# Moving one group of small matmuls behind the KV stage, and three more no-op matmuls, in a fused attention and FFN kernel

## Chip, cores, metric

One core of a Trainium2 chip. The time is the device time of one execution in microseconds (us); lower is better. Profiles are of one execution each. The profiled execution of the kernel before was a slow one, with a granted clock of the tensor engine of 0.655 and 1249.2 us.

## The reference

```python
def reference(A_x, A_wqkv, A_wo, B_x, B_w_gate, B_w_up, B_w_down, c, w_mod):
    # _A_ref: qkv = x @ wqkv, 32 heads of 32; phi(t) = where(t > 0, t + 1, exp(t)) + 1e-6
    #   kv = sum_s phi(k) v ; z = sum_s phi(k) ; o = phi(q) kv / (phi(q) z + 1e-6) ; o @ wo
    # _B_ref: (silu(x @ w_gate) * (x @ w_up)) @ w_down
    x = A_x                                               # 2048 x 1024
    mod = (_silu(c) @ w_mod).reshape(c.shape[0], 6, 1, -1)
    sa, ca, ga, sb, cb, gb = ...                          # six rows of 1024
    h = _layernorm(x, axis=-1) * (1 + ca) + sa
    x = x + ga * _A_ref(h, A_wqkv, A_wo)
    h = _layernorm(x, axis=-1) * (1 + cb) + sb
    x = x + gb * _B_ref(h, B_w_gate, B_w_up, B_w_down)
    return x
```

The last four modulation rows (ga, gb, sb, cb) are not needed until the end of the attention half. The kernel makes them, in two groups, in between other matmuls.

## The kernel before

The 2048 rows are worked in four chunks of 512 (`sc` 0 to 3). A chunk's K stage is eight groups of eight matmuls (128x128 weights, 512 columns). The KV stage of the chunk before, 128 matmuls of 64 columns, stands behind the first two groups.

```python
    def kv_phase(sc):                       # 128 matmuls of 64 columns
        kvp = acc_b("kvp", (HG, 2, DH))
        for hg in range(HG):
            for t in range(STC):
                for i in range(HPC):
                    mm(kvp[i * DH:(i + 1) * DH, hg, :, :], lhsT=pks[sc][...], rhs=v_ones(...), ...)
        ...

    def mod_load(cols):                     # four loads of 1 MB
        blks = []
        for lo in cols:
            t = big("wml", [DC, NB])
            nc.sync.dma_start(out=t[:], in_=wm_v[:, :, lo:lo + NB])
            blks.append(t)
        return blks

    def mod_rows(blks):                     # 32 matmuls, four at a time side by side
        ps = acc_b("modr")
        for j in range(DC):
            for g in range(4):
                mm(ps[32 * g:32 * g + 32, :], lhsT=sc32[:, j, :], rhs=blks[g][:, j, :], ...)
        ...

    def keep_warm(acc, n):                  # no-ops: they multiply by zeros
        for _ in range(n):
            mm(acc[:], lhsT=sel[:, 0, :], rhs=sel[:], start=True, stop=True)
    ...
    keep_warm(spare, 9)
    ...                                     # first modulation rows, transposes, more no-ops
    for sc in range(NSC):
        if sc > 0:
            k_phase(sc, 0, 2)
            kv_phase(sc - 1)
            k_phase(sc, 2, 4)
            if sc >= 2:
                mod_spread(sc - 2, mod_rows(blks))
            k_phase(sc, 4, 8)
            if sc == 1:
                blks = mod_load([2 * D, 2 * D + NB, 5 * D, 5 * D + NB])
            if sc == 2:
                blks = mod_load([3 * D, 3 * D + NB, 4 * D, 4 * D + NB])
        v_phase(sc)
        ...                                 # layernorm of the next chunk, behind phi of K group 3
```

In the profile, `kvp` is the KV stage, `modr` the modulation rows of the second kind, `wml` their weights, `sel` the no-ops' operand, and `acc<-wk,hT` the K stage.

## Time and profile before

| | before |
|---|---|
| time, median of 3 (range) | 837.8 us (837.59 to 838.01) |
| profiled execution | 1249.2 us, a slow one |

The first fence has lines of the profile's page: busy time of each engine with its share of the span, and the chain that ended last by engine. The second is the view of cores. The third is the waits of the tensor engine: total us, times, longest us.

```profile
PE 1232.9 (99%) x4560; PEld 468.0 (37%) x4641; DVE 309.5 (25%) x598; ACT 169.3 (14%) x253; POOL 60.8 (5%) x167
...
PE 99%; issue 1%; DVE 0%
```

```profile
core 0: 1249.2 us, clock 0.655
```

```profile
PE acc L98 <- issue: 5.1, 26, 0.2
PE acc L98 <- DVE sel L429: 1.2, 1, 1.2
```

PE is the limit from end to end, and it waits for 6.3 us in all. But this is an execution at 0.655 of the clock, half as long again as the timed ones. Here are its KV stages of chunks 1 and 2 in the timeline of PE (start us, us, engine, line, operation, tiles, shapes, count, and in brackets the idle time just before):

```profile
86.15 1.42 PE L98 MATMUL kvp<-v,pk 128*32 128x64 bf16 x128
87.51 15.83 PE L98 MATMUL acc<-wk,hT 128*128 128x512 bf16 x47
...
129.35 1.42 PE L98 MATMUL kvp<-v,pk 128*32 128x64 bf16 x128
130.97 5.05 PE L98 MATMUL acc<-wk,hT 128*128 128x512 bf16 x15 [0.20 <-issue]
135.95 2.77 PE L98 MATMUL modr<-wml,sc 128*32 128x512 bf16 x32
```

### The profile page before, as it was taken

How to read it: one execution, taken by the hardware profiler on the slowest of the kernel's cores; microseconds unless marked ns; L12 is line 12 of the kernel's file. 1: busy time of each engine (PE TensorE's matmuls, PEld its weight loads, DVE VectorE, ACT ScalarE, POOL GpSimd, SP SyncE). 2: the span in 40 equal slices, each digit the busy share in tenths (PEclk: the TensorE clock that was granted, in tenths of full speed). 3: DMA queues.
4: the chain of work that ended last, by engine and by line, in shares of the span. 5: the costliest groups of instructions: out<-in, count | busy, mean ns of one | idle time of the engine just before them, and what ended most of it. 6: DMA issues, size and time to landing. Idle time of an engine off the chain costs nothing.

```text
span 1249.2 us, 11163 instructions
## 1 busy us (share of the span) xinstructions
PE 1232.9 (99%) x4560; PEld 468.0 (37%) x4641; DVE 309.5 (25%) x598; ACT 169.3 (14%) x253; POOL 60.8 (5%) x167
## 2 busy tenths in 40 slices
PE   9999999999999999999999999999999999999998
PEld 3333333333433333333333333333333333333333
DVE  4443531564221222311111232111112221111111
ACT  2423322322011101001111000011100001111000
POOL 1101200110300001000000000000000000000000
PEclk7666666666666666666666666666666666666666
DMA  9444520139452414253140231623204218300011
GB/s 344 120 152 135 148 65 1 36 108 307 111 149 87 167 47 160 64 165 105 34 140 30 72 122 58 218 69 98 71 1 143 76 49 271 124 11 1 13 38 34
DMA packets 126756, 129.33 MB, mean 104 GB/s; under 512 B 34033, under 2 KB 108273, under 8 KB 126193
## 3 DMA queue, kind: packets, MB, share of 16 engines
q1 hardware_dynamic: 122368, 114.97, 29.3%
q0 software_dynamic: 4048, 13.25, 3.4%
q8 instruction: 36, 0.59, 0.2%
q10 hardware_dynamic: 288, 0.40, 0.1%
q14 instruction: 16, 0.12, 0.0%
HBM read 108.53 MB, written 12.72 MB: 97 GB/s over the span
## 4 chain that ended last, share of the span: by engine, by line
PE 99%; issue 1%; DVE 0%
PE acc L98 90%; PE a_ps L98 7%; PE modr L98 0%; PE kvp L98 0%; PE mod_ps L98 0%; PE tp L101 0%; PE den L98 0%; PE wf L98 0%; DVE e L638 0%; DVE ob L641 0%; DVE sel L429 0%; DVE neg_half L172 0%
## 5 line engine op out<-in xcount | busy, mean ns | idle before, releaser
L98 PE MATMUL acc<-h2T,wgu 128*128 128x512 bf16 x1756 | 580.8, 513 | 5.0 <-issue 1.6
L98 PEld LDWEIGHTS <-wgu 128*128 128x128 bf16 x1792 | 217.1, 121 | 367.4 <-issue 367.1
L98 PE MATMUL acc<-wd,gu 128*128 128x512 bf16 (+2 forms) x908 | 293.5, 503 | 2.4 <-issue 1.0
L617 DVE TENSOR_TENSOR gu<-acc,e 128x512 bf16<-128x512 f32 x112 | 77.5, 692 | 497.9 <-PE acc L98 475.4
L98 PEld LDWEIGHTS <-gu 128*128 128x128 bf16 x924 | 111.0, 121 | 182.1 <-issue 178.6
L616 ACT ACTIVATE e<-acc 128x512 f32<-128x512 f32 x112 | 66.9, 597 | 607.0 <-PE acc L98 588.5
L98 PEld LDWEIGHTS <-hT 128*128 128x128 bf16 x512 | 61.6, 121 | 102.9 <-issue 100.6
L98 PE MATMUL a_ps<-wo,pq 128*128 128x512 bf16 x250 | 85.1, 512 | 0.6
L98 PE MATMUL acc<-wk,hT 128*128 128x512 bf16 x248 | 83.7, 513 | 1.3 <-issue 0.8
L98 PE MATMUL acc<-hT,wq 128*128 128x512 bf16 x247 | 83.0, 512 | 1.6 <-issue 1.4
L98 PE MATMUL acc<-wv,hT 128*128 128x512 bf16 x251 | 83.5, 513 | 0.8 <-issue 0.4
L638 DVE TENSOR_TENSOR e<-acc,gb_bc 128x512 f32<-128x512 f32 (+2 forms) x33 | 22.3, 676 | 232.8 <-PE acc L98 219.7
L288 ACT ACTIVATE eb<-acc 128x512 bf16<-128x512 f32 x64 | 38.0, 597 | 131.8 <-PE acc L98 131.0
L289 DVE TENSOR_SCALAR eb<-eb 128x512 bf16<-128x512 bf16 x64 | 18.8, 293 | 134.0 <-ACT eb L288 133.9
L98 PEld LDWEIGHTS <-pq 128*128 128x128 bf16 x256 | 30.8, 120 | 52.6 <-issue 52.6
L98 PEld LDWEIGHTS <-wq 128*128 128x128 bf16 x256 | 29.9, 119 | 51.5 <-issue 51.2
L227 ACT ACTIVATE xn<-x,nmr,rstd 128x1024 bf16<-128x1024 f32 x16 | 19.8, 1239 | 191.9 <-POOL nmr L225 191.9
L585 POOL DMA_DIRECT2D x_scratch<-x x16 | 9.7, 608 | 657.5 <-DVE x L578 657.5
L578 DVE TENSOR_TENSOR x<-a_ps,x_sb 128x512 f32<-128x512 f32 x32 | 22.1, 692 | 35.7 <-PE a_ps L98 33.3
L326 ACT CAST v<-acc 128x512 bf16<-128x512 f32 x32 | 18.7, 584 | 57.0 <-PE acc L98 55.4
L211 POOL TENSOR_TENSOR rstd<-veps,neg_half 128x1 f32<-128x1 f32 x32 | 17.8, 555 | 103.0 <-DVE veps L209 102.9
L641 DVE TENSOR_TENSOR ob<-e,x1r 128x512 bf16<-128x512 f32 (+2 forms) x33 | 22.3, 675 | 1.0
(76 smaller groups left out, 268.4 us busy)
## 6 DMA issues: line engine op xcount, KB each, us to landing
wgu<-in_B_w_gate_dram SPq DMA_DIRECT2D x28, 1024.0 KB, 5.5
wgu<-in_B_w_up_dram SPq DMA_DIRECT2D x28, 1024.0 KB, 6.0
x_sb<-in_A_x_dram SPq DMA_DIRECT2D x32, 256.0 KB, 6.0
wml<-in_w_mod_dram SPq DMA_DIRECT2D x8, 1024.0 KB, 8.5
x_scratch<-x POOLq DMA_DIRECT2D x16, 512.0 KB, 2.9
x1r<-x_scratch SPq DMA_DIRECT2D x31, 256.0 KB, 2.8
wd<-in_B_w_down_dram SPq DMA_DIRECT2D x7, 1024.0 KB, 5.7
rbc<-rden_scratch POOLq DMA_DIRECT2D x16, 256.0 KB, 4.6
```

The costliest lines, as they stand in the source:

```text
L98: return tc.keep_in_program_order(nc.tensor.matmul(out, lhsT=lhsT, rhs=rhs, start=start, stop=stop))
L211: nc.gpsimd.tensor_tensor(out=rstd[:, 0:n], in0=veps[:, 0:n], in1=neg_half[:].to_broadcast([P, n]), op=ALU.pow)
L227: nc.scalar.activation(out=dst, in_=src, func=ACT.Identity, bias=nmr[:], scale=rstd[:, 0:1])
L288: nc.scalar.activation(out=e[:], in_=acc, func=ACT.Exp)
L289: nc.vector.tensor_scalar(out=e[:], in0=e[:], scalar1=1.0, scalar2=PHI_EPS, op0=ALU.min, op1=ALU.add)
L326: nc.scalar.copy(out=v[:, t * D + nb * NB:t * D + (nb + 1) * NB], in_=acc[:])
L578: nc.vector.tensor_tensor(out=x1[:, ns], in0=a_ps[:], in1=x_t[:, ns], op=ALU.add)
L585: nc.gpsimd.dma_start(out=x1_dram[st * P:(st + 1) * P, :], in_=x1[:])
L616: nc.scalar.activation(out=sg[:], in_=ps[0][:], func=ACT.Silu)
L617: gm = nc.vector.tensor_tensor(out=guT[sc][f // GPT][:, f % GPT, :], in0=ps[1][:], in1=sg[:], op=ALU.mult)
L638: nc.vector.tensor_tensor(out=yt, in0=y_ps, in1=gb_bc[:, ns], op=ALU.mult)
L641: nc.vector.tensor_tensor(out=ob, in0=yt, in1=x1r, op=ALU.add)
```

## The change

The three no-ops were to fill gaps among the first loads. The first group of modulation rows was to go behind the KV stage, both of them being made of narrow matmuls, and to be done earlier.

```diff
-        keep_warm(spare, 2)
+        keep_warm(spare, 4)
         pe_transpose_tile(hT, xns[2], 2)
         mod_rows_a(2)
-        keep_warm(spare, 5)
+        keep_warm(spare, 6)
         mod_rows_a(3)
 ...
             k_phase(sc, 0, 2)
             kv_phase(sc - 1)
+            if sc == 2:
+                mod_spread(0, mod_rows(blks))
             k_phase(sc, 2, 4)
-            if sc >= 2:
-                mod_spread(sc - 2, mod_rows(blks))
+            if sc == 3:
+                mod_spread(1, mod_rows(blks))
             k_phase(sc, 4, 8)
```

## The prediction

> **What bounds it.** The tensor engine, start to end: PE 1232.9 of 1249.2 us (99%) on the page, a chain of waits that is 99% PE, and only 6.3 us of waits of PE, the longest 1.2. But this profile is a slow execution: granted clock 0.655 (view of cores), while timed runs take 837.8. Estimate for full clock: PE part (1249-16-3) x 0.655 = 806 us, 16 us of start, 3 of tail[...]: 832 to 835. So at most 3 to 6 us of PE stalls hide in the timed runs, which caps any gain.
>
> **What the change does.** (a) Three more no-op 128x512 matmuls: two before the third input tile's transposes, one before the last modulation rows. (b) The 32 column-tiled matmuls of the first modulation rows move two K groups earlier, directly behind the 128 KV matmuls. The order of instructions shows the same loads in the same SP order, and DVE, ACT and POOL reordered around chunk 2.
>
> **(a), costed.** The first no-ops take 0.427 us each (timeline)[...]; later ones 0.33 to 0.38[...]. In the trace the third tile's normalisation ends at 11.86 us and its transposes start at 11.91; at full clock PE is free for about 0.5 us before, so two no-ops (0.43) cost nothing. The last rows begin at 14.88, right as five no-ops end; their weights land by about 13.6 (7.8 after the issue at 5.8). At full clock the no-ops end near 13.9, so the sixth costs up to 0.2 us. [...]
>
> **(b), costed.** PE work is unchanged: 1.42 (KV) + 2.77 us (rows). The 0.20 us gap between KV and the next K group may go: -0.1. The cost is on DVE: the next chunk's layernorm may start only after the phi of K group 3. Before, the rows (about 1.8 us at full clock) stood between groups 3 and 4 and gave DVE a window with no evacuation; after, the window lies where layernorm is not yet allowed. Four phis (0.98 each) plus statistics (about 1.65 a tile) are 10.5 us of DVE against 6.9 of PE. Chunk 3's normalised input comes about 1.8 us later relative to PE. In the slow trace it is modulated by 156.5 and used at 169.9; at full clock I reckon 2 to 4 us of slack before, 0.5 to 2.5 after: just enough, as in chunk 1, which has this pattern already. The gate rows' earlier landing buys nothing: the multiplication of wo waits for wo's own load.
>
> **Prediction: 837.7 us, 8 in 10 between 836.0 and 839.3.** Faster by over 2%: 0.01; within 2%: 0.98; slower: 0.01.
>
> **What shows it.** PE still 99% busy; first real K matmul within 0.3 us of before; rows directly after KV with no idle; chunk 3's statistics begin about 1.8 us (fast) or 2.8 (slow) later relative to the end of the K stage; no PE wait at chunk 3's K stage; the chain stays PE.
>
> **What would make it wrong.** If the timed runs lose the full tensor clock in the first 16 us, which the slow profile hides, the no-ops could win 1 to 3 us. If chunk 3's input is already late at full clock, (b) costs up to 2 us. A fast profile would decide.

Its sum for full clock came to 832 to 835 us with a term of about 7 us that does not scale. That term is cut: the terms that stand, 806, 16 and 3, come to 825, and the 3 to 6 us of hidden stalls rested on the longer sum. The forecast of 837.7 does not use the sum; it lies 0.1 under the timed 837.8. In the profile after, the no-ops start 0.22 us apart from 5.19 us on.

## More of the kernel before

Only fast ones are compared.

Every matmul is two instructions, a weight load and the multiplication (4644 of each on the page after). So a KV stage is 256 instructions.

## The result, and the profile after

| | before | after |
|---|---|---|
| time, median of 4 (range) | 837.69 us (837.27 to 838.01) | 839.49 us (839.28 to 839.62) |
| ratio, 95% interval | | 1.0022 (1.0004 to 1.0039) |
| span of a profile at full clock | 836.0 us (run e0) | 837.4 us |

Ratios are the mean time of one kernel's fast runs over that of the other's of the same rounds, so not quite the ratio of the medians. The change costs 1.8 us, 0.2%. The prediction was 837.7, at most 839.3.

Lines of the page after: busy time, the chain, and the DMA queue that carries instructions (packets, MB, share of 16 engines' time).

```profile
PE 829.2 (99%) x4644; PEld 378.9 (45%) x4644; DVE 308.1 (37%) x598; ACT 169.0 (20%) x253; POOL 61.1 (7%) x167
...
q8 instruction: 36, 0.59, 0.3%
...
PE 98%; DMA 1%; DVE 0%; issue 0%; SPq 0%; ACT 0%
```

The view of cores and the waits of PE:

```profile
core 0: 837.4 us, clock 1.000
```

```profile
PE mod_ps L98 <- DMA wme<-in_w_mod_dram: 1.7, 2, 1.4
PE acc L98 <- DVE sel L429: 1.2, 1, 1.2
PE modr L98 <- issue: 1.1, 1, 1.1
PE acc L98 <- issue: 0.9, 1, 0.9
```

The wait for the first weights (`mod_ps`) is at the start of the kernel, and the kernel before has it too at full clock (2.0 us in run e0). Two others are new against the slow profile, both called "issue": for nothing that the profile shows. The timeline of PE says where they are:

```profile
61.79 1.22 PE L98 MATMUL kvp<-v,pk 128*32 128x64 bf16 x128
62.94 1.90 PE L98 MATMUL acc<-wk,hT 128*128 128x512 bf16 x8
65.73 8.79 PE L98 MATMUL acc<-wk,hT 128*128 128x512 bf16 x40 [0.89 <-issue]
...
91.72 1.22 PE L98 MATMUL kvp<-v,pk 128*32 128x64 bf16 x128
92.75 0.63 PE L98 MATMUL modr<-wml,sc 128*32 128x512 bf16 x8
94.43 1.48 PE L98 MATMUL modr<-wml,sc 128*32 128x512 bf16 x24 [1.05 <-issue]
```

Both stand 8 matmuls behind a KV stage. The second is in the middle of the modulation rows, which read four loads (their last packet began at 65.46 us) and write one accumulator, so no data can be missing there. This trace has every matmul's record (4644, of as many weight loads). Counted from the first no-op, 957 matmuls and weight loads have begun before the first idle stretch and 1468 before the second. One semaphore wait of PE's sequencer lies between, so they are 512 instructions apart, twice 256. In the packed traces of all runs that idle here, the count is the same: 479 weight loads have begun before the idle stretch of chunk 1 and 734 before that of chunk 2, whatever work stands there.

And 0.59 MB in 36 packets are 16 KB each; 36 times 256 is 9216, and PE's matmuls and weight loads are 9288. In the packet records of the changed kernel each of the 36 has 16384 bytes, and they come 254 of PE's instructions apart in the mean (209 have begun at the first, at 17.87 us, 9103 at the last, at 819.93). With the 512 between the idle stretches, I take one packet for a block of 256 instructions of PE's program. In the packet records of the trace one instruction packet runs from 63.30 to 64.39 and one from 92.05 to 93.02; PE resumes 1.34 and 1.41 us after their ends. A short window of the DMA view around the first (63.2 to 64.5 us: packets, MB, share) shows it among the loads:

```profile
q1 hardware_dynamic: 204, 0.20, 47.3%
q8 instruction: 1, 0.02, 5.2%
```

So the theory (F in the runs): PE's program is fetched a block ahead. In the changed kernel the packet of the block that PE needed after instruction 957 began when 945 had begun (63.30 us), and the next one at 67.35 us, when 973 had begun, so after that border. How much of its program PE can hold, no run tests. The 256 short instructions of a KV stage last 1.15 us, and a block takes 2.4 us from the start of its packet until PE goes on with it (2.3 to 2.9 in all the traces in which PE waits). A border that falls just behind the start of a KV stage leaves too little work until the next. The rivals: D, my prediction's, that the layernorm of the next chunk comes late; W, that the no-ops matter by their time or by the rate of PE's early matmuls (in the changed kernel the first eight no-ops start 0.43 us apart, those from 5.19 us on 0.22); later S, that the sequencer asks late whatever the DMA queues hold.

### The profile page after: what moved, and what is told of

Read it like the earlier page. It is cut to its first block, busy times and chain, and to the rows that moved or that the text cites. A ratio compares the mean times of both kernels' runs of the same rounds, so it can differ in the third digit from the quotient of the medians.

```text
span 837.4 us, 11251 instructions
## 1 busy us (share of the span) xinstructions
PE 829.2 (99%) x4644; PEld 378.9 (45%) x4644; DVE 308.1 (37%) x598; ACT 169.0 (20%) x253; POOL 61.1 (7%) x167
## 4 chain that ended last, share of the span: by engine, by line
PE 98%; DMA 1%; DVE 0%; issue 0%; SPq 0%; ACT 0%
PE acc L98 89%; PE a_ps L98 7%; DMA wme<-in_w_mod_dram 1%; PE kvp L98 1%; PE modr L98 0%; PE mod_ps L98 0%; PE den L98 0%; PE tp L101 0%; SPq L120 0%; DVE wo L550 0%; PE wf L98 0%; SPq L134 0%; DVE pq L291 0%; ACT eb L288 0%; DVE eb L289 0%
## 5 line engine op out<-in xcount | busy, mean ns | idle before, releaser
L98 PE MATMUL acc<-h2T,wgu 128*128 128x512 bf16 x1792 | 387.6, 379 | 0.0
L98 PEld LDWEIGHTS <-wgu 128*128 128x128 bf16 x1792 | 175.2, 98 | 211.3
L98 PE MATMUL acc<-wd,gu 128*128 128x512 bf16 (+2 forms) x924 | 196.1, 373 | 0.0
L619 DVE TENSOR_TENSOR gu<-acc,e 128x512 bf16<-128x512 f32 x112 | 77.5, 692 | 299.2 <-PE acc L98 299.2
L98 PEld LDWEIGHTS <-gu 128*128 128x128 bf16 x924 | 89.3, 98 | 104.5
L98 PEld LDWEIGHTS <-hT 128*128 128x128 bf16 x512 | 49.7, 98 | 60.9 <-issue 1.6
L98 PE MATMUL acc<-wk,hT 128*128 128x512 bf16 x256 | 57.1, 379 | 0.9 <-issue 0.9
L98 PE MATMUL a_ps<-wo,pq 128*128 128x512 bf16 x256 | 57.4, 379 | 0.0
L98 PE MATMUL acc<-hT,wq 128*128 128x512 bf16 x256 | 56.8, 379 | 0.0
L98 PE MATMUL acc<-wv,hT 128*128 128x512 bf16 x256 | 55.9, 379 | 0.0
L581 DVE BATCH_NORM_STATS2 stats<-x 128x6 f32<-128x512 f32 x32 | 22.2, 695 | 1.1
```

What stands on the lines that cost most here:

```text
L98: return tc.keep_in_program_order(nc.tensor.matmul(out, lhsT=lhsT, rhs=rhs, start=start, stop=stop))
L581: nc.vector.bn_stats(out=stats[:, nb, :], in_=x1[:, ns])
L619: gm = nc.vector.tensor_tensor(out=guT[sc][f // GPT][:, f % GPT, :], in0=ps[1][:], in1=sg[:], op=ALU.mult)
```

## The experiments

All ten kernels gave correct results. The runs had 5 rounds, with the kernel before in each; its medians were 837.75 (e0 to e3), 837.83 (e4 to e7) and 837.75 (e8, e9). The intervals are about 0.13% each way. So the verdicts on parts of a microsecond rest on the idle stretches in the traces, and the times confirm their sum; by the times alone, e1, e7 and e8 are not clear of the kernel before. Traces of the runs miss a few matmul records, one at a time; a count of 7 or 15 with 0.16 us idle behind it is such a place (e0's in chunk 2, for one) and is given as "none".

| run | what | median us | ratio (95%) | idle in chunk 1 | idle in chunk 2 |
|---|---|---|---|---|---|
| e0 | before | 837.49 | 0.9997 (0.9985 to 1.001) | 0.43 | none |
| e1 | no-ops alone | 838.64 | 1.001 (0.9998 to 1.0023) | 1.07 | none |
| e2 | rows alone | 838.93 | 1.0014 (1.0001 to 1.0026) | 0.56 | 0.93 |
| e3 | after, borders moved by 96 | 837.26 | 0.9994 (0.998 to 1.0007) | none | none |
| e4 | before, borders moved by 20 | 842.62 | 1.0057 (1.0044 to 1.0069) | 2.93 | 1.3 (1.61 shown, one record missing) |
| e5 | before, borders moved by 96 | 837.36 | 0.9997 (0.9985 to 1.001) | none | none |
| e6 | the same, at a later place | 837.54 | 0.9996 (0.9984 to 1.0009) | none | none |
| e7 | after, three first no-ops fewer | 838.61 | 1.001 (0.9997 to 1.0024) | 0.52 | 1.24 |
| e8 | after, first loads later | 838.00 | 1.0004 (0.9991 to 1.0016) | none | 0.55 |
| e9 | after, both groups of loads later | 837.34 | 1.0 (0.9986 to 1.0013) | none | none |

### e0: the kernel before, at full clock

No edit.

> The kernel before again, for a trace at full clock. Theory F (instruction fetch: the tensor engine reads its program in blocks of 256 instructions, one block ahead, and the 256 short instructions of a KV stage use up a block faster than the next one comes): 837.7 us; in chunk 1 an idle stretch of about 0.3 us some 11 matmuls after the KV stage; none after the KV stage of chunk 2. Rival D (the layernorm of the next chunk is late, as I predicted): no idle stretch behind the KV stages at all, and more than 0.5 us of slack before the K stage of chunk 3.

```profile
61.84 1.22 PE L98 MATMUL kvp<-v,pk 128*32 128x64 bf16 x128
63.00 2.55 PE L98 MATMUL acc<-wk,hT 128*128 128x512 bf16 x10
65.97 8.15 PE L98 MATMUL acc<-wk,hT 128*128 128x512 bf16 x37 [0.43 <-issue]
...
91.31 1.22 PE L98 MATMUL kvp<-v,pk 128*32 128x64 bf16 x128
92.69 3.40 PE L98 MATMUL acc<-wk,hT 128*128 128x512 bf16 x15 [0.16 <-DMA wml<-in_w_mod_dram]
96.03 1.91 PE L98 MATMUL modr<-wml,sc 128*32 128x512 bf16 x32
```

As F expected; its blocks are the 16 KB packets above, 254 instructions from one to the next. The kernel before loses 0.43 us at the same count of instructions: its KV stage begins six earlier, so the border falls 11 matmuls behind it (10 recorded). The slow profile had nothing there, and its packet records say why: the same block's packet runs from 82.56 to 83.92 us, before the KV stage begins at 86.15, the modulation loads being over by 77.5. So it is with chunk 2 (125.33 to 126.56, KV stage at 129.35). PE was slow and the loads were not (their 1 KB records take 46 ns in both traces, median), so here the fetch met empty queues; in e0 the packet begins 1.4 us after the start of the KV stage.

The traces' idle stretches account for the spans: 0.89 + 1.05 after, 0.43 before, a difference of 1.51 us, against 837.4 - 836.0 = 1.4 us. The medians differ by 1.8: the profiled run was the fastest of the kernel after (839.28) and the slowest of e0 (837.86).

### e1: the no-ops alone

```diff
-        keep_warm(spare, 2)
+        keep_warm(spare, 4)
 ...
-        keep_warm(spare, 5)
+        keep_warm(spare, 6)
```

> The three no-ops alone. Theory F: six more instructions ahead move every block border six instructions earlier against the work, so chunk 1 idles about 0.9 us, 8 matmuls after its KV stage, instead of 0.3; chunk 2 does not idle; 838.3 to 838.6 us with up to 0.2 us in the first 16 us. Rival D: at most 0.2 us over before. Rival W (warmth of the tensor clock): equal to or under before.

```profile
61.88 1.22 PE L98 MATMUL kvp<-v,pk 128*32 128x64 bf16 x128
63.03 1.90 PE L98 MATMUL acc<-wk,hT 128*128 128x512 bf16 x7
66.01 8.79 PE L98 MATMUL acc<-wk,hT 128*128 128x512 bf16 x40 [1.07 <-DVE eb L289]
```

838.64 us, 0.9 over before and just over the range given. The no-ops cost nothing where they stand: the first K matmul begins at 15.62 us against 15.58 in e0. They cost 47 us later, by moving the program six instructions against the borders of its blocks. That the profile names DVE as what ended this wait is an inference from what happened at that moment; the same wait is "issue" in other runs.

### e2: the rows alone

```diff
+            if sc == 2:
+                mod_spread(0, mod_rows(blks))
             k_phase(sc, 2, 4)
-            if sc >= 2:
-                mod_spread(sc - 2, mod_rows(blks))
+            if sc == 3:
+                mod_spread(1, mod_rows(blks))
```

> The moved modulation rows alone. Theory F: chunk 1 as before (0.3 us), and an idle stretch of about 0.9 us inside the rows of chunk 2, after 11 of their 32 matmuls; 838.4 to 838.8 us. Rival D: 0 to 2 us over before, and what idles is the start of chunk 3's K stage, not the rows.

```profile
91.39 1.22 PE L98 MATMUL kvp<-v,pk 128*32 128x64 bf16 x128
92.43 0.83 PE L98 MATMUL modr<-wml,sc 128*32 128x512 bf16 x11
94.19 1.47 PE L98 MATMUL modr<-wml,sc 128*32 128x512 bf16 x21 [0.93 <-issue]
```

838.93 us, 0.1 over the range given, with the idle stretch after 11 rows, as expected. Before, 11 K matmuls (2.4 us at 0.216 each, as the 64 of a V stage take 13.81 us in the changed kernel) stood between the KV stage and this border and covered the fetch. Eleven rows last 0.83 us and do not. Rival D falls: PE does not wait at the K stage of chunk 3.

### e3: the changed kernel with its borders moved

```diff
-    def keep_warm(acc, n):
+    def keep_warm(acc, n, w=NB):
         for _ in range(n):
-            mm(acc[:], lhsT=sel[:, 0, :], rhs=sel[:], start=True, stop=True)
+            mm(acc[:, 0:w], lhsT=sel[:, 0, :], rhs=sel[:].rearrange("p h e -> p (h e)")[:, 0:w], start=True, stop=True)
 ...
-    keep_warm(spare, 9)
+    keep_warm(spare, 57, 81)
```

> The changed kernel with its first nine no-ops of 512 columns made into 57 of 81 columns: nearly the same columns, 96 more instructions in the queue, which puts the block borders into the middle of each KV stage. Theory F: both idle stretches (0.89 us in chunk 1, 1.05 us inside the rows) are gone and the time is 837.3 to 837.8 us. Rival D, or any theory in which the rows' place or the no-ops' time costs: 839.3 to 839.7 us, as the changed kernel.

```profile
62.05 1.22 PE L98 MATMUL kvp<-v,pk 128*32 128x64 bf16 x128
63.21 10.53 PE L98 MATMUL acc<-wk,hT 128*128 128x512 bf16 x47
...
91.97 1.92 PE L98 MATMUL modr<-wml,sc 128*32 128x512 bf16 x32
```

837.26 us: all of the loss is gone, with the rows and the no-ops where the change put them. Only the first nine no-ops are cut smaller.

### e4: the kernel before with its borders moved by 20

```diff
-    keep_warm(spare, 9)
+    keep_warm(spare, 19, 243)
```

(`keep_warm` as in e3.)

> The kernel before with its first nine no-ops of 512 columns made into 19 of 243: the same columns and 20 more instructions, so that the block border falls 2 instructions behind the start of the KV stages of chunks 1 and 2 instead of 22. Theory F: idle stretches one matmul after the KV stage, about 2.4 us in chunk 1 (0.43 before) and about 1.4 us in chunk 2 (none before, where the block had been asked for 0.9 us earlier than in chunk 1); 840.3 to 841.8 us. Rival (order or DVE): 837.5 as before, nothing else having changed.

```profile
62.62 0.39 PE L98 MATMUL acc<-wk,hT 128*128 128x512 bf16 x1
65.94 11.78 PE L98 MATMUL acc<-wk,hT 128*128 128x512 bf16 x46 [2.93 <-issue]
...
94.91 1.22 PE L98 MATMUL kvp<-v,pk 128*32 128x64 bf16 x128
97.75 3.41 PE L98 MATMUL acc<-wk,hT 128*128 128x512 bf16 x15 [1.61 <-DMA wml<-in_w_mod_dram]
```

Twenty instructions without work cost 4.8 us. The place, one matmul behind the KV stage, was right. (That a block is "asked for" earlier in chunk 2 is read from where its packet begins: in the changed kernel 1.51 us behind the start of the KV stage in chunk 1 and 0.33 in chunk 2.) In chunk 1 the size given was low (2.4 us). In chunk 2 some 0.3 of the 1.61 us is the matmul behind the KV stage, whose record is missing (its weight load is at 96.06), so 1.3 against the 1.4 expected. The time, 842.62, is over the range given, by a second cost. After the idle 2.93 us the tensor clock is down for a while (in the trace at half speed from 65.93 to 69.34), as the windows view shows (start:end, us, busy us of PE, PEld, DVE, ACT, POOL, granted clock, DMA share, GB/s):

```profile
65.94:77.55 11.61, 11.61 (x46) 4.93 (x46) 7.03 (x18) 3.09 (x5) 0.95 (x4) 0.85 0.01 3
77.55:91.37 13.82, 13.71 (x64) 6.26 (x65) 6.42 (x19) 8.78 (x13) 2.37 (x6) 1.00 0.69 172
```

In the first 3 us of it the weight loads come every 0.43 us instead of 0.22. So this run lost the full clock after 2.93 us of idling. Three of the five runs had a mean clock of 0.996 to 0.998 and took 842.6 to 844.2 us, two had 1.000 and took 841.2, inside the range.

### e5 and e6: the kernel before with its borders moved by 96

e5 makes the first no-ops `keep_warm(spare, 57, 81)`, as e3. e6 instead makes the five no-ops before the last rows 53 of 48 columns.

> The kernel before with 96 more instructions in its first no-ops, columns nearly the same. Theory F: the 0.43 us in chunk 1 is gone, the first K matmul is up to 0.25 us later as in e3; 837.0 to 837.4 us. It tells whether the moved rows have a worth of their own once the borders are out of the way: e3, with rows moved, had 837.26.

> The kernel before, with the five no-ops ahead of the last modulation rows made into 53 of 48 columns: 96 more instructions, later. Theory F: no idle stretch in chunk 1 and no later start of K; 836.9 to 837.3 us, the best so far by a little.

837.36 and 837.54 us, no idle stretch behind a KV stage in either. e6 missed its range by 0.2: K began at 15.89 us instead of 15.58. The narrow no-ops took 1.50 us where five wide ones take 1.25, but PE was 0.26 us late when they began (12.93, 12.67 in e0), so which of the two cost it is not shown. e5 and e3 do not differ, so the rows' new place is worth nothing that these runs resolve once the borders are out of the way. Nor do e3, e5 and e6 beat before beyond the intervals; 0.43 us is all that they can win.

### e7: the changed kernel with three first no-ops fewer

```diff
-    keep_warm(spare, 9)
+    keep_warm(spare, 6)
```

> The changed kernel with six instead of nine first no-ops: the three new ones stay where they are, but the count of instructions ahead of the chunks is that of before. Theory F: as e2, 0.4 to 0.6 us idle in chunk 1 and 0.9 us inside the rows after 11 of them; 838.6 to 839.0 us. If the new no-ops cost by their time or place: 839.5 as the changed kernel.

```profile
66.12 8.15 PE L98 MATMUL acc<-wk,hT 128*128 128x512 bf16 x37 [0.52 <-issue]
...
94.56 1.47 PE L98 MATMUL modr<-wml,sc 128*32 128x512 bf16 x21 [1.24 <-issue]
```

838.61 us, 0.52 us idle in chunk 1, and an idle stretch in the rows after 11 of them, as e2, but of 1.24 us instead of the 0.9 expected (the profiled run was the slowest of the five, 839.41). The three new no-ops are still there. What they cost, they cost by their number, and three others taken away give it back.

### e8 and e9: the same borders, with the queues empty

In chunk 1 the packet of the missing block began about 63.3 us in e0 (63.28), e1 (63.38), e2 (63.46) and after (63.30), though the no-ops and rows had moved the work against the border. That is about when the first four modulation weight loads run out (95% of their records in the changed kernel have begun by 63.3). So what the block waits for could be the DMA queues. In e8 the loads are made to wait for the KV sums of chunk 1; in e9 the second group waits for those of chunk 2 in the same way. One load of each held group still goes early (49.07 in e8, 49.58 and 84.12 in e9); the other three start at 63.92 in e8 and at 64.23 and 93.11 in e9, or later.

```diff
-    def mod_load(cols):
+    def mod_load(cols, gate=False):
 ...
             t = big("wml", [DC, NB])
+            if gate and not blks:
+                nc.vector.tensor_copy(out=t[:, 0, 0:1], in_=kv_acc[:, 0, 0:1])
 ...
             kv_phase(sc - 1)
+            if sc == 1:
+                blks = mod_load([2 * D, 2 * D + NB, 5 * D, 5 * D + NB], gate=True)
 ...
             k_phase(sc, 4, 8)
-            if sc == 1:
-                blks = mod_load([2 * D, 2 * D + NB, 5 * D, 5 * D + NB])
```

> The changed kernel with the first four modulation weight loads (4 MB) held back, but for one of the four, until DVE has taken the KV sums of chunk 1 (one copy of 128x1 makes the load wait); borders of blocks and order of PE are as in the changed kernel. Theory Q (the missing block of instructions stands in the DMA queues behind these loads): in chunk 1 its packet, which began 1.5 us after the start of the KV stage, begins at least 0.8 us earlier, the idle stretch of 0.89 us there falls under 0.2, and the time is 838.4 to 838.8 us. Rival S (the sequencer asks for the block late, whatever the queues hold): packet and idle stretch as in the changed kernel, 839.2 to 839.7 us.

> As e8, and the second four loads held back in the same way until the KV sums of chunk 2. Theory Q: the idle stretch of 1.05 us inside the modulation rows falls too, to under 0.4 us, and the time is 837.3 to 838.0 us with the borders where the changed kernel has them. Rival S: 839.2 to 839.7 us. Either way a later K stage of chunk 3 would show the loads themselves coming too late.

The windows view before and in the KV stage of chunk 1, first of the changed kernel, then of e8 (the two last columns are DMA share and GB/s):

```profile
60.00:61.10 1.10, 1.10 (x7) 0.51 (x6) 1.09 (x3) 0.60 (x1) 0.00 (x0) 1.00 1.10 351
61.80:63.00 1.20, 1.20 (x130) 1.16 (x130) 0.46 (x3) 0.60 (x1) 0.00 (x0) 1.00 1.09 345
```

```profile
60.00:61.10 1.10, 1.10 (x7) 0.51 (x6) 1.07 (x4) 0.58 (x1) 0.00 (x0) 1.00 0.05 15
61.60:63.00 1.40, 1.40 (x130) 1.24 (x131) 0.66 (x3) 0.60 (x1) 0.00 (x0) 1.00 0.00 0
```

In e8 the only packet between 60.0 and 61.1 us is the block of instructions. It runs from 60.07 to 61.00, 3.2 us earlier than in the changed kernel (3.0 against the start of the KV stage) and before the KV stage begins. The DMA view of that window:

```profile
DMA packets 1, 0.02 MB, mean 15 GB/s; under 512 B 0, under 2 KB 0, under 8 KB 0
q8 instruction: 1, 0.02, 5.3%
```

The timeline of PE in e8, and in e9:

```profile
61.60 1.22 PE L98 MATMUL kvp<-v,pk 128*32 128x64 bf16 x128
62.76 10.53 PE L98 MATMUL acc<-wk,hT 128*128 128x512 bf16 x47
...
91.52 0.63 PE L98 MATMUL modr<-wml,sc 128*32 128x512 bf16 x8
92.70 1.48 PE L98 MATMUL modr<-wml,sc 128*32 128x512 bf16 x24 [0.55 <-issue]
```

```profile
91.83 1.92 PE L98 MATMUL modr<-wml,sc 128*32 128x512 bf16 x32
```

Rival S falls. With the borders of the changed kernel, the idle stretch of chunk 1 is gone in e8 and that of the rows in e9, at 838.0 and 837.34 us. e8 came in under its range: the stretch in chunk 2 halved as well, its packet beginning at 90.34, just before the KV stage, instead of 0.33 us behind its start. Why the second group's loads let it through earlier there was not tried. Each of these two kernels had one or two runs 1 to 2 us longer than its others (839.05 and 838.67; 839.48), and so had before (838.84, 838.69); their cause is open.

In what way the block's packet waits while the loads are in the queues, no run here shows.

## Why the prediction was wrong

- **The range.** It was missed by 0.19 us, the centre by 1.8.
- **The step that failed: "PE work is unchanged: 1.42 (KV) + 2.77 us (rows)", and from it only "-0.1" for PE.** The work is unchanged, but PE also has to be fed with instructions. The rows took the place of the 11 long matmuls under which the next block was fetched. Measured: 0.93 us alone (e2), 1.05 us in the whole change.
- **The second step that failed: "so two no-ops (0.43) cost nothing".** They and the sixth do cost nothing in the first 16 us; even the "up to 0.2 us" was too much, as PE waited 0.35 us there for weights in e0. But six instructions move the borders: 0.43 us idle in chunk 1 became 0.89 (e1: 1.07).
- **What was right.** The gap of DVE moved as said: the statistics of chunk 3 begin 7.08 us before the end of the K stage in e0 (97.70 and 104.78) and 5.14 in the changed kernel (101.07 and 106.21), 1.9 us later against 1.8 predicted. The input itself lost more: its modulation begins 5.2 us before the K stage of chunk 3 in e0 (113.38 and 118.60) and 2.1 in the changed kernel (117.92 and 120.03), and there ends 0.6 us after that stage has begun, where the prediction left 0.5 to 2.5 us of slack. PE still does not wait, as it takes the eight pieces one after the other. The bound by PE, the small scale and "within 2%" held.
- **What it could have seen.** It named the slow profile as a risk, but thought of the clock in the first 16 us (1.00 from 4.38 us on in the profile after). The slow clock hid the kernel's own 0.43 us instead: PE came to its KV stage after the loads were over and the block was there. The 256 instructions of a KV stage and the 36 instruction packets of 16 KB on the page were there to be put together.

Settled by runs: where the borders are decides (e3, e4, e7), and so does what stands in the DMA queues at that time (e8, e9). Open: why the idle stretches of one kernel differ by 0.1 to 0.3 us between runs (1.05 in the changed kernel, 1.24 in e7, where more covers it), and the two points left open above.

## What to carry to other kernels

In this kernel a dense run of 256 very short tensor-engine instructions outran the fetch of the program: it lasted 1.15 us, and a block took 2.4 us from the start of its packet until use. Put long matmuls behind it, not more short ones (in chunk 2, eleven long ones, 2.4 us, left no idle stretch in e0; eleven rows, 0.83 us, left 0.93 us in e2). And don't fill the DMA queues with large loads just ahead of it (with three of four loads held back, the packet came 3.2 us earlier in e8). When a no-op or a reordering moves the time by parts of a microsecond far from its place (47 us in e1), count the instructions between the idle stretches and look for the fetch's packets; and judge from a profile at the clock of the timed runs.
